# First FFN in 64-row tiles, groups of four chunk pairs, o copied by halves on ScalarE, and a new start, in a fused convolution and FFN

## The chip, the cores and the metric

One core of one Trainium2 chip. The time is device microseconds of the whole launch, the median of several runs. The profile comes from one such run; its span is about 1 to 2 us below the time of its run. PE is the tensor engine, DVE the vector engine, ACT the scalar engine, POOL the general one, SP the engine that issues many of the transfers. A ratio of two kernels is the mean time of one kernel's runs over that of the other's in the same rounds, so it is not quite the ratio of the medians quoted beside it.

## The reference

```python
# x: 8 x 4096 x 192, weight_gen: 8 x 4096 x 8 heads x 7 taps, w_in: 192 x 2048, w_out: 2048 x 192
w = softmax(weight_gen, axis=-1)
y[b, s, h, :] = sum_k w[b, s, h, k] * x_padded[b, s + k, h, :]     # causal, 24 channels a head
out = (relu(y @ w_in) ** 2) @ w_out                                # float32, 32768 tokens
```

## The kernel before

Tokens go in 64 blocks of 512. For a block: a band matrix per head is made on DVE (`st_band`), the convolution is a product of x with it on PE (`st_conv`, into a PSUM tile `yp`), ACT copies it to `y`. The first FFN has 2048 outputs in 16 chunks of 128, taken as 8 chunk pairs; each pair has a PSUM tile `h` of two banks, one for each half of the tokens. ACT makes the relu (`t`), DVE the square (`g`), and the second FFN adds `g` times `w_out` into a PSUM tile `o` of two banks, again one for each token half. There are three buffers for `h` and `yp` together and one for `o`; these fill the eight banks. The softmax runs in slices beside it, one batch ahead.

```python
    ps_h = ctx.enter_context(tc.tile_pool(name="ps_h", bufs=3, space=bass.MemoryType.PSUM))
    ps_o = ctx.enter_context(tc.tile_pool(name="ps_o", bufs=1, space=bass.MemoryType.PSUM))
    ...
    def st_mm1_lower(j, fps):            # rows 0 to 127 of w_in
        ...
                for half in range(2):
                    nc.tensor.matmul(
                        out=h[:, half, jj, :],
                        lhsT=w_a[:, fc * P : (fc + 1) * P],
                        rhs=y[:, half * TH : (half + 1) * TH], ...
    def st_mm1_upper(j, fps):            # rows 128 to 191, two row tiles at once
        ...
                for half, r0 in enumerate((0, LO)):
                    nc.tensor.matmul(
                        out=h_t[(j, fp)][:, half, jj, :],
                        lhsT=w_b[r0 : r0 + LO, fc * P : (fc + 1) * P],
                        rhs=y[r0 : r0 + LO, TB : TB + TH], ...
                        tile_position=(r0, 0),
    ...
    def st_o_evac(j):                    # one copy of all of o, on DVE
        o_sb = p_os.tile([P, 2, 2 * Dm], f32, name="o_sb")
        nc.vector.tensor_copy(out=o_sb, in_=o_t[j][:, :, 0 : 2 * Dm])
        nc.sync.dma_start(...)
    ...
    G0, G1, G2 = (0, 1, 2), (3, 4, 5), (6, 7)
    LATE = (5, 6, 7)
    # the loop over blocks, PE's part of it:
            st_mm1_lower(j, G0); st_mm1_upper(j, G0)
            if j: st_mm2(j - 1, LATE)
            ...
            st_mm1_lower(j, G1); st_mm1_upper(j, G1)
            st_mm2(j, (0, 1, 2))
            ...
            st_mm1_lower(j, G2)
            st_conv(j + 1); st_y_evac(j + 1)
            st_mm1_upper(j, G2)
            st_mm2(j, (3, 4))
```

The softmax here doesn't subtract the row's maximum and nothing guards it: scores larger than these inputs give would overflow.

## Time and profile before

| | before |
|---|---|
| time, median | 820.3 us |
| PE, DVE, ACT busy | 96%, 78%, 68% of the span |
| block period in the middle | 12.144 us |
| first FFN matmul starts | 24.25 us |
| 64 block periods / all the rest | 777 us / 43 us |

The block period is the distance between the first convolution matmuls of two blocks, from the matmuls' starts in the trace, between 120 and 780 us. PE's busy share alone would not tell a reader what can be gained; the starts of the matmuls do. The lines are in the prediction below.

### The profile page before, as it was taken

How to read it: one execution, taken by the hardware profiler on the slowest of the kernel's cores; microseconds unless marked ns; L12 is line 12 of the kernel's file. 1: busy time of each engine (PE TensorE's matmuls, PEld its weight loads, DVE VectorE, ACT ScalarE, POOL GpSimd, SP SyncE). 2: the span in 40 equal slices, each digit the busy share in tenths (PEclk: the TensorE clock that was granted, in tenths of full speed). 3: DMA queues.
4: the chain of work that ended last, by engine and by line, in shares of the span. 5: the costliest groups of instructions: out<-in, count | busy, mean ns of one | idle time of the engine just before them, and what ended most of it. 6: DMA issues, size and time to landing. Idle time of an engine off the chain costs nothing.

```text
span 819.6 us, 27464 instructions
## 1 busy us (share of the span) xinstructions
PE 783.1 (96%) x12288; PEld 662.1 (81%) x12288; DVE 642.0 (78%) x1194; ACT 557.1 (68%) x628; POOL 90.4 (11%) x126
## 2 busy tenths in 40 slices
PE   0499999999999999999999999999999999999997
PEld 0278888888888888888888888888888888888886
DVE  3498878878888878887788877887788887676674
ACT  1377677766777767777776767777677776676665
POOL 7650100010000000001000010001000000000000
PEclk9799999999999999999999999999999999999999
DMA  5844443345333353433533344233433334333111
GB/s 117 166 73 82 104 91 66 50 71 140 53 69 61 65 135 61 71 51 79 133 50 65 67 118 83 60 53 69 137 67 58 61 69 80 61 71 50 46 40 40
DMA packets 123799, 63.17 MB, mean 77 GB/s; under 512 B 87713, under 2 KB 121120, under 8 KB 122912
## 3 DMA queue, kind: packets, MB, share of 16 engines
q0 software_dynamic: 44480, 17.57, 19.6%
q1 hardware_dynamic: 79200, 43.84, 18.6%
q8 instruction: 96, 1.57, 0.8%
q14 instruction: 23, 0.19, 0.1%
HBM read 49.60 MB, written 29.36 MB: 96 GB/s over the span
## 4 chain that ended last, share of the span: by engine, by line
PE 94%; DVE 1%; DMA 1%; ACT 1%; POOL 0%; issue 0%; SPq 0%; ACTq 0%; DVEq 0%
PE o L322 43%; PE h L291 27%; PE h L304 16%; PE yp L266 7%; DMA wg<-in_weight_gen_dram 1%; ACT t L333 0%; DVE o_sb L343 0%; DVE bd L229 0%; ACT ex L142 0%; DVE g L339 0%; POOL v_small L163 0%; DVE ssum L150 0%; DVE rcp L155 0%; SPq L177 0%; ACTq L142 0%
## 5 line engine op out<-in xcount | busy, mean ns | idle before, releaser
L333 ACT ACTIVATE t<-h 128x1024 f16<-128x1024 f32 x512 | 490.0, 1026 | 128.7 <-PE h L304 128.7
L339 DVE TENSOR_TENSOR g<-t 128x1024 f16<-128x1024 f16 x512 | 353.9, 692 | 144.2 <-ACT t L333 139.3
L322 PE MATMUL o<-w_o,g 128*128 128x192 f16 x4096 | 371.5, 247 | 1.5 <-DVE o_sb L343 1.5
L322 PEld LDWEIGHTS <-g 128*128 128x128 f16 x4096 | 328.4, 98 | 42.0 <-issue 35.5
L291 PE MATMUL h<-y,w_a 128*128 128x256 f16 x2048 | 260.9, 274 | 9.6 <-ACT t L333 8.7
L291 PEld LDWEIGHTS <-w_a 128*128 128x128 f16 x2048 | 197.7, 98 | 34.1 <-issue 10.4
L229 DVE TENSOR_TENSOR bd<-wr,mask 128x832 f16<-128x832 f16 (+2 forms) x320 | 170.8, 583 | 10.6 <-POOL mask L94 8.4
L304 PE MATMUL h<-y,w_b 64*128 64x256 f16 x2048 | 146.4, 273 | 0.0
L279 ACT CAST y<-yp 128x768 f16<-128x768 f32 x64 | 51.1, 798 | 113.7 <-PE yp L266 113.7
L304 PEld LDWEIGHTS <-w_b 64*128 64x128 f16 x2048 | 84.7, 95 | 41.9 <-issue 27.6
L218 POOL DMA_DIRECT2D xt<-in_x_dram x56 | 48.4, 864 | 564.0 <-PE yp L266 518.2
L266 PE MATMUL yp<-bd,xt 128*32 128x104 f16 (+14 forms) x4096 | 65.9, 209 | 20.8 <-DVE bd L229 20.7
L266 PEld LDWEIGHTS <-xt 128*32 128x32 f16 (+3 forms) x4096 | 54.2, 91 | 34.7 <-issue 23.7
L343 DVE COPY o_sb<-o 128x768 f32<-128x768 f32 x64 | 60.8, 950 | 1.0 <-PE o L322 1.0
L150 DVE TENSOR_REDUCE ssum<-ex 128x64 f32<-128x448 f32 (+4 forms) x51 | 26.3, 515 | 13.4 <-ACT ex L142 13.3
L142 ACT ACTIVATE ex<-wg 128x448 f32<-128x448 f32 (+4 forms) x51 | 27.5, 540 | 13.1 <-DMA wg<-in_weight_gen_dram 13.1
L163 DVE TENSOR_TENSOR v_big<-ex,rcp 128x112 f16<-128x112 f32 (+3 forms) x188 | 32.7, 236 | 1.6
L155 DVE RECIPROCAL rcp<-ssum 128x64 f32<-128x64 f32 (+4 forms) x51 | 23.9, 469 | 1.8
L163 POOL TENSOR_TENSOR v_small<-ex,rcp 128x84 f16<-128x84 f32 (+1 forms) x28 | 13.8, 523 | 18.1 <-ACT t L333 14.1
L210 POOL DMA_DIRECT2D xt<-in_x_dram x8 | 4.6, 580 | 78.4 <-PE yp L266 67.7
L90 POOL TENSOR_SCALAR_AFFINE_SELECT mask<-mask 128x208 f16<-128x208 f16 (+2 forms) x6 | 6.9, 1146 | 0.4
L94 POOL TENSOR_SCALAR_AFFINE_SELECT mask<-mask 128x208 f16<-128x208 f16 (+2 forms) x6 | 6.6, 1093 | 0.4
(15 smaller groups left out, 16.2 us busy)
## 6 DMA issues: line engine op xcount, KB each, us to landing
out_dram<-o_sb SPq DMA_DIRECT2D x64, 384.0 KB, 2.8
xt<-in_x_dram POOLq DMA_DIRECT2D x56, 240.0 KB, 4.2
wg<-in_weight_gen_dram SPq DMA_DIRECT2D x6, 1064.0 KB, 7.1
wr<-vd SPq DMA_DIRECT2D x56, 80.0 KB, 3.0
vd<-v_big SPq DMA_DIRECT2D x7, 512.0 KB, 4.1
wg<-in_weight_gen_dram SPq DMA_DIRECT2D x4, 392.0 KB, 6.1
xt<-in_x_dram POOLq DMA_DIRECT2D x8, 192.0 KB, 3.7
wg<-in_weight_gen_dram SPq DMA_DIRECT2D x1, 896.0 KB, 5.9
```

The costliest lines, as they stand in the source:

```text
L142: nc.scalar.activation(out=self.ex[:, lo:hi].rearrange("p r g k e -> p (r g) k e"), in_=self.wg[:, lo:hi].rearrange("p r (g e) k -> p (r g ...
L163: eng.tensor_tensor(out=bass.AP(tensor=v.tensor, offset=v.offset + lo * H * SL + lo % SL * 2 + g * SL * 2, ap=[list(v.ap[0]), [H * SL + 2, ...
L218: eng.dma_start(out=dst, in_=rows(src, t0 + BASE, width))
L229: nc.vector.tensor_tensor(out=bd_t[j][:, H * lo : H * hi].rearrange("p (g m c) -> p g m c", g=HP, c=2 * SL), in0=wr_t[j][:, i].unsqueeze(2 ...
L266: nc.tensor.matmul(out=yp[p0 : p0 + m, ci, col : col + b - a], lhsT=x_t[j][:, i, 32 * q : 32 * q + m], rhs=bd[:, h // 2, h % 2, a - lo : b ...
L279: nc.scalar.copy(out=y, in_=yp_t[j].rearrange("p a c -> p (a c)")[:, 0 : TB + TH])
L291: nc.tensor.matmul(out=h[:, half, jj, :], lhsT=w_a[:, fc * P : (fc + 1) * P], rhs=y[:, half * TH : (half + 1) * TH], start=(jj == 0), stop ...
L304: nc.tensor.matmul(out=h_t[(j, fp)][:, half, jj, :], lhsT=w_b[r0 : r0 + LO, fc * P : (fc + 1) * P], rhs=y[r0 : r0 + LO, TB : TB + TH], sta ...
L322: nc.tensor.matmul(out=o[:, half, cc * Dm : (cc + 1) * Dm], lhsT=g_t[(j, fp)][:, half, jj, cc * P : (cc + 1) * P], rhs=w_o[:, fc, :], star ...
L333: nc.scalar.activation(out=t1, in_=h_t[(j, fp)], func=ActF.Relu)
L339: nc.vector.tensor_tensor(out=g, in0=t1, in1=t1, op=AluOp.mult)
L343: nc.vector.tensor_copy(out=o_sb, in_=o_t[j][:, :, 0 : 2 * Dm])
```

## The change

Its intent: every matmul of the first FFN in 64-row tiles, so that chunk pairs need no change of mode between two parts; groups of four pairs instead of three, three and two; the copy of `o` moved from busy DVE to ACT, by token halves, each as soon as its half is complete; and a start that loads weights sooner, splits the first softmax in three and runs 48 matmuls of zeros to bring PE's clock up.

```diff
-    p_t1 = ctx.enter_context(tc.tile_pool(name="p_t1", bufs=4))
-    p_g = ctx.enter_context(tc.tile_pool(name="p_g", bufs=6))
+    p_t1 = ctx.enter_context(tc.tile_pool(name="p_t1", bufs=6))
+    p_g = ctx.enter_context(tc.tile_pool(name="p_g", bufs=10))
...
+    def st_mm1(j, fp):
+        h = ps_h.tile([P, 2, 2, TH], f32, name="h", tag="h")
+        h_t[(j, fp)] = h
+        for jj in range(2):
+            fc = 2 * fp + jj
+            for k in range(NK):                          # NK = 3
+                for half, r0 in enumerate((0, RT)):      # RT = 64
+                    nc.tensor.matmul(
+                        out=h[:, half, jj, :],
+                        lhsT=w_i[r0 : r0 + RT, k, fc * P : (fc + 1) * P],
+                        rhs=y_t[j][r0 : r0 + RT, k, :],
+                        start=(jj == 0 and k == 0), stop=(k == NK - 1),
+                        tile_position=(r0, 0), ...
...
+    G0, G1 = (0, 1, 2, 3), (4, 5, 6, 7)
+        for i in range(48):                              # before the first block
+            nc.tensor.matmul(out=wp[:, 0:TB], lhsT=warm[:, 0:P], rhs=warm, ...)
...
+        for j in range(NBLK):
+            late = j in (0, 2)
+            ...            st_conv(j + 1); st_y_evac(j + 1)
+            for fp in G0:
+                st_mm1(j, fp); st_relu(j, fp); st_sq(j, fp)
+            if j:
+                for half in (0, 1):
+                    st_mm2(j - 1, G1, (half,))
+                    o_copy(j - 1, half, nc.scalar.copy)
+                o_store(j - 1, (0, 1), nc.sync)
+            ...            # bands of block j + 2, the softmax part
+            for fp in G1:
+                st_mm1(j, fp); st_relu(j, fp); st_sq(j, fp)
+            st_mm2(j, G0)
+            if late:
+                st_bands(j + 2, BANDS)
```

The convolution is laid out so that `y` has rows of 64 in each half, with 72 matmuls in place of 64. Cut: the loading of `w_in` into 64 rows and its copy to the other 64, one band mask for all tiles, the softmax in parts of 8, 8 and 16 rows.

More of the change, by code (lines that the diff above doesn't have):

```diff
@@ L49 @@
     TH = TB // 2
+    RT = 64
+    NK = D // RT
     NT = 5
@@ L55 @@
     bounds = [0, 104, 208, 304, 400, TB]
+    shifts = [lo - s for lo, s in zip(bounds, starts)]
     AluOp = mybir.AluOpType
@@ L73, with band_mask, copy_w_in @@
     ps_o = ctx.enter_context(tc.tile_pool(name="ps_o", bufs=1, space=bass.MemoryType.PSUM))
-    w_a = const.tile([P, Dff], f16, name="w_a")
-    w_b = const.tile([P, Dff], f16, name="w_b")
+    w_i = const.tile([P, NK, Dff], f16, name="w_i")
     w_o = const.tile([P, NF, Dm], f16, name="w_o")
-    mask = const.tile([P, TB, 2], f16, name="mask")
-    mask0 = const.tile([P, bounds[1], 2], f16, name="mask0")
-    R0 = 8
-    v_big = const.tile([P, R + 2 * (KK - 1), HP, SL, 2], f16, name="v_big")
-    v_small = [
-        const.tile([P, R0 + 2 * (KK - 1), HP, SL, 2], f16, name=f"v_small{i}") for i in range(2)
-    ]
-    def band_mask(t, shift):
-        n = t.shape[1]
-        nc.gpsimd.memset(t, 1.0)
-        nc.gpsimd.affine_select(
-            out=t, in_=t, pattern=[[1, n], [0, 2]], compare_op=AluOp.is_ge, fill=0.0,
-            base=shift, channel_multiplier=-1,
-        )
-        nc.gpsimd.affine_select(
-            out=t, in_=t, pattern=[[-1, n], [0, 2]], compare_op=AluOp.is_ge, fill=0.0,
-            base=KK - 1 - shift, channel_multiplier=1,
-        )
-    def load_w_in():
-        nc.gpsimd.dma_start(out=w_a, in_=moe_w_in[0:P, :])
-        for r0 in (0, LO):
-            nc.gpsimd.dma_start(out=w_b[r0 : r0 + LO, :], in_=moe_w_in[P:D, :])
+    mask = const.tile([P, P, 2], f16, name="mask")
+    FIRST = (8, 8, 16)
+    v_big = const.tile([P, R + 2 * HALO, HP, SL, 2], f16, name="v_big")
+    v_first = [
+        const.tile([P, r + 2 * HALO, HP, SL, 2], f16, name=f"v_first{i}")
+        for i, r in enumerate(FIRST)
+    ]
+    def band_mask():
+        nc.gpsimd.memset(mask, 1.0)
+        for sign, base in ((1, 0), (-1, KK - 1)):
+            nc.gpsimd.affine_select(
+                out=mask, in_=mask, pattern=[[sign, P], [0, 2]], compare_op=AluOp.is_ge,
+                fill=0.0, base=base, channel_multiplier=-sign,
+            )
+    WQ = 4
+    def load_w_in():
+        src = moe_w_in.rearrange("(k p) f -> p k f", p=RT)
+        for q in range(WQ):
+            c = slice(q * Dff // WQ, (q + 1) * Dff // WQ)
+            nc.gpsimd.dma_start(out=w_i[0:RT, :, c], in_=src[:, :, c])
+    def copy_w_in(q):
+        c = slice(q * Dff // WQ, (q + 1) * Dff // WQ)
+        nc.sync.dma_start(out=w_i[RT:P, :, c], in_=w_i[0:RT, :, c])
     def load_w_out():
@@ L186, in new_vd @@
         return vd_t[b]
-    x_t, wr_t, bd_t, yp_t, y_t, g_t, h_t, t1_t, o_t = ({} for _ in range(9))
+    x_t, wr_t, bd_t, yp_t, y_t, g_t, h_t, t1_t, o_t, o_sb_t = ({} for _ in range(10))
     def rows(ap2d, t0, width):
@@ L196, in rows, with block_load, x_load, wr_load @@
         )
-    def st_load(j):
-        b, t0 = j // NBB, (j % NBB) * TB
-        xt = p_x.tile([P, NT, D], f16, name="xt")
-        wr = p_wr.tile([P, NT, HP, SL * 2], f16, name="wr")
-        x_t[j], wr_t[j] = xt, wr
-        wr2 = wr.rearrange("p t g c -> p t (g c)")
-        vd = vd_t[b]
-        for dst, src, width, eng in (
-            (wr2, vd, H * SL, nc.sync),
-            (xt, x[b], D, nc.gpsimd),
-        ):
-            if t0 == 0:
-                eng.dma_start(out=dst[:, 0], in_=src[0:P, :])
-                first = rows(src, BASE + STEP, width)
-                first = bass.AP(
-                    tensor=first.tensor, offset=first.offset,
-                    ap=[first.ap[0], [STEP * width, NT - 1], first.ap[2]],
-                )
-                eng.dma_start(out=dst[:, 1:NT], in_=first)
-            else:
-                eng.dma_start(out=dst, in_=rows(src, t0 + BASE, width))
+    def block_load(j, dst, src, width, eng):
+        t0 = (j % NBB) * TB
+        if t0 == 0:
+            eng.dma_start(out=dst[:, 0], in_=src[0:P, :])
+            later = rows(src, BASE + STEP, width)
+            later = bass.AP(
+                tensor=later.tensor, offset=later.offset,
+                ap=[later.ap[0], [STEP * width, NT - 1], later.ap[2]],
+            )
+            eng.dma_start(out=dst[:, 1:NT], in_=later)
+        else:
+            eng.dma_start(out=dst, in_=rows(src, t0 + BASE, width))
+    def x_load(j):
+        x_t[j] = p_x.tile([P, NT, D], f16, name="xt")
+        block_load(j, x_t[j], x[j // NBB], D, nc.gpsimd)
+    def wr_load(j):
+        wr_t[j] = p_wr.tile([P, NT, HP, SL * 2], f16, name="wr")
+        block_load(
+            j, wr_t[j].rearrange("p t g c -> p t (g c)"), vd_t[j // NBB], H * SL, nc.sync
+        )
     def st_band(j, i):
@@ L224, in st_band @@
         n = hi - lo
-        m = mask[:, lo:hi]
-        if i == 0 and j % NBB == 0:
-            m = mask0
+        shift = 0 if i == 0 and j % NBB == 0 else shifts[i]
+        m = mask[:, shift : shift + n]
         shape = (P, HP, n // SL, 2 * SL)
@@ L242, in conv_pieces @@
     def conv_pieces():
-        for i in range(NT):
-            lo, hi = bounds[i], bounds[i + 1]
-            for later in (True, False):
-                for q in range(4):
-                    yield later, i, q, 32 * q, 0, lo, lo, hi
-                for half in (0, 1):
-                    a, b = max(lo, TH * half), min(hi, TH * (half + 1))
-                    if a < b:
-                        for q in (4, 5):
-                            yield later, i, q, 32 * (q - 4) + LO * half, 1, a - TH * half, a, b
+        pieces = []
+        for half in (0, 1):
+            a, b = TH * half, TH * (half + 1)
+            pieces.append([
+                (i, half, max(bounds[i], a), min(bounds[i + 1], b))
+                for i in range(NT) if bounds[i] < b and bounds[i + 1] > a
+            ])
+        for pair in zip(*pieces):
+            for later in (True, False):
+                for q in range(0, 2 * NK, 2):
+                    for i, half, a, b in pair:
+                        for qq in (q, q + 1):
+                            yield later, i, qq, half, a, b
     def st_conv_alloc(j):
-        yp_t[j] = ps_h.tile([P, 2, TB], f32, name="yp", tag="h")
+        yp_t[j] = ps_h.tile([P, 2 * TB], f32, name="yp", tag="h")
     def st_conv(j):
-        yp = yp_t[j]
-        for later, i, q, p0, ci, col, a, b in conv_pieces():
+        for later, i, q, half, a, b in conv_pieces():
             lo, hi = bounds[i], bounds[i + 1]
@@ L265, in st_conv @@
             bd = bd_t[j][:, H * lo : H * hi].rearrange("p (g c e) -> p g e c", g=HP, e=2)
+            p0 = RT * half + 32 * (q % 2)
+            col = TH * (q // 2) - TH * half
             nc.tensor.matmul(
-                out=yp[p0 : p0 + m, ci, col : col + b - a],
+                out=yp_t[j][p0 : p0 + m, col + a : col + b],
                 lhsT=x_t[j][:, i, 32 * q : 32 * q + m],
@@ L276, in st_y_evac, with st_mm2 @@
     def st_y_evac(j):
-        y = p_y.tile([P, TB + TH], f16, name="y")
+        y = p_y.tile([P, NK, TH], f16, name="y")
         y_t[j] = y
-        nc.scalar.copy(out=y, in_=yp_t[j].rearrange("p a c -> p (a c)")[:, 0 : TB + TH])
-    def st_mm1_lower(j, fps):
-        y = y_t[j]
-        for fp in fps:
-            h = ps_h.tile([P, 2, 2, TH], f32, name="h", tag="h")
-            h_t[(j, fp)] = h
-            for jj in range(2):
-                fc = 2 * fp + jj
-                for half in range(2):
+        nc.scalar.copy(
+            out=y, in_=yp_t[j][:, 0 : NK * TH].rearrange("p (k c) -> p k c", k=NK)
+        )
+    def st_mm1(j, fp):
[5 more added lines that the diff above has]
+                for half, r0 in enumerate((0, RT)):
                     nc.tensor.matmul(
                         out=h[:, half, jj, :],
-                        lhsT=w_a[:, fc * P : (fc + 1) * P],
-                        rhs=y[:, half * TH : (half + 1) * TH],
-                        start=(jj == 0), stop=False, skip_group_check=True,
-                    )
-    def st_mm1_upper(j, fps):
-        y = y_t[j]
-        for fp in fps:
-            for jj in range(2):
-                fc = 2 * fp + jj
-                for half, r0 in enumerate((0, LO)):
-                    nc.tensor.matmul(
-                        out=h_t[(j, fp)][:, half, jj, :],
-                        lhsT=w_b[r0 : r0 + LO, fc * P : (fc + 1) * P],
-                        rhs=y[r0 : r0 + LO, TB : TB + TH],
-                        start=False, stop=(jj == 1), skip_group_check=True,
+                        lhsT=w_i[r0 : r0 + RT, k, fc * P : (fc + 1) * P],
+                        rhs=y_t[j][r0 : r0 + RT, k, :],
+                        start=(jj == 0 and k == 0), stop=(k == NK - 1),
+                        skip_group_check=True,
                         tile_position=(r0, 0),
                     )
-    def st_mm2(j, fps):
+    def st_mm2(j, fps, halves=(0, 1)):
         if fps[0] == 0:
@@ L319, in st_mm2 @@
                 fc = 2 * fp + jj
-                for c in range(TB // P):
-                    half, cc = c // 2, c % 2
-                    nc.tensor.matmul(
-                        out=o[:, half, cc * Dm : (cc + 1) * Dm],
-                        lhsT=g_t[(j, fp)][:, half, jj, cc * P : (cc + 1) * P],
-                        rhs=w_o[:, fc, :],
-                        start=(fc == 0 and cc == 0), stop=(fc == NF - 1),
-                        skip_group_check=True,
-                    )
+                for half in halves:
+                    for cc in range(2):
+                        nc.tensor.matmul(
+                            out=o[:, half, cc * Dm : (cc + 1) * Dm],
+                            lhsT=g_t[(j, fp)][:, half, jj, cc * P : (cc + 1) * P],
+                            rhs=w_o[:, fc, :],
+                            start=(fc == 0 and cc == 0), stop=(fc == NF - 1),
+                            skip_group_check=True,
+                        )
     def st_relu(j, fp):
@@ L339, in st_sq @@
         nc.vector.tensor_tensor(out=g, in0=t1, in1=t1, op=AluOp.mult)
-    def st_o_evac(j):
-        o_sb = p_os.tile([P, 2, 2 * Dm], f32, name="o_sb")
-        nc.vector.tensor_copy(out=o_sb, in_=o_t[j][:, :, 0 : 2 * Dm])
-        nc.sync.dma_start(
-            out=out[j * TB : (j + 1) * TB, :].rearrange("(c p) d -> p c d", p=P),
-            in_=o_sb.rearrange("p a (b d) -> p (a b) d", b=2),
-        )
-    def softmax_whole(s, engines):
-        s.exp(0, s.rh)
-        s.recip(0, s.rh)
-        for n, lo in enumerate(range(0, s.rh, SL)):
-            s.scale(lo, min(lo + SL, s.rh), engines[n % len(engines)])
-        s.store(nc.sync)
@@ L358, with o_copy, o_store @@
-    G0, G1, G2 = (0, 1, 2), (3, 4, 5), (6, 7)
-    LATE = (5, 6, 7)
+    def o_copy(j, half, copy):
+        if half == 0:
+            o_sb_t[j] = p_os.tile([P, 2, 2 * Dm], f32, name="o_sb")
+        copy(out=o_sb_t[j][:, half], in_=o_t[j][:, half, 0 : 2 * Dm])
+    def o_store(j, halves, eng):
+        n = len(halves) * TH
+        t0 = j * TB + halves[0] * TH
+        eng.dma_start(
+            out=out[t0 : t0 + n, :].rearrange("(c p) d -> p c d", p=P),
+            in_=o_sb_t[j][:, halves[0] : halves[-1] + 1].rearrange(
+                "p a (b d) -> p (a b) d", b=2
+            ),
+        )
@@ L360, with st_bands @@
+    def st_bands(j, tiles):
+        if j < NBLK:
+            for i in tiles:
+                st_band(j, i)
+    G0, G1 = (0, 1, 2, 3), (4, 5, 6, 7)
     UNIT = 4
+    BANDS = (0, 2, 1, 3, 4)
     with nc.allow_low_precision("fp16 matmul pipeline"), tc.manual_schedule():
         vd0 = new_vd(0)
-        parts = [Softmax(0, P * R0 * i, R0, v_small[i % 2], vd0) for i in range(S // (P * R0))]
-        parts[0].load(nc.sync)
-        nc.vector.memset(v_small[0], 0.0)
-        band_mask(mask0, 0)
@@ L369 @@
-        softmax_whole(parts[0], (nc.vector, nc.gpsimd))
-        st_load(0)
-        load_w_in()
-        for i in range(1, NT):
-            band_mask(mask[:, bounds[i] : bounds[i + 1]], bounds[i] - starts[i])
-        parts[1].load(nc.sync)
-        st_load(1)
-        nc.vector.memset(v_small[1], 0.0)
-        for i in range(NT):
-            st_band(0, i)
+        parts = [
+            Softmax(0, P * sum(FIRST[:i]), r, v_first[i], vd0) for i, r in enumerate(FIRST)
+        ]
+        warm = const.tile([P, TB], f16, name="warm")
@@ new lines @@
+        nc.vector.memset(warm, 0.0)
+        for i in (0, 1):
+            parts[i].load(nc.sync)
+            nc.vector.memset(v_first[i], 0.0)
+        wp = ps_h.tile([P, 2 * TB], f32, name="wp", tag="h")
+        for i in range(48):
+            nc.tensor.matmul(
+                out=wp[:, 0:TB], lhsT=warm[:, 0:P], rhs=warm, start=True, stop=True
+            )
+        x_load(0)
+        load_w_in()
+        band_mask()
+        for i in (0, 1):
+            s = parts[i]
+            s.exp(0, s.rh)
+            s.recip(0, s.rh)
+            s.scale(0, s.rh, nc.vector)
+            s.store(nc.sync)
+            if i == 0:
+                wr_load(0)
+                wr_load(1)
+                copy_w_in(0)
+                copy_w_in(1)
@@ L379 @@
+        copy_w_in(2)
+        copy_w_in(3)
+        parts[2].load(nc.sync)
+        x_load(1)
+        load_w_out()
+        st_bands(0, BANDS)
         st_conv_alloc(0)
@@ L381 @@
         st_y_evac(0)
-        load_w_out()
-        band_mask(mask[:, 0 : bounds[1]], -starts[0])
-        softmax_whole(parts[1], (nc.gpsimd,))
-        for s in parts[2:]:
-            s.load(nc.sync)
-        st_load(2)
-        nc.vector.memset(v_big, 0.0)
-        nxt, done = None, 0
-        if B > 1:
-            nxt = Softmax(1, 0, R, v_big, new_vd(1))
-            nxt.load(nc.sync)
-        for j in range(NBLK):
-            b, jb = j // NBB, j % NBB
-            more = j + 1 < NBLK
-            if j < 2:
-                softmax_whole(parts[2 + j], (nc.gpsimd,))
-            if nxt and jb == 5:
-                nxt.store(nc.sync)
-                nxt, done = None, 0
-                if b + 2 < B:
-                    nxt = Softmax(b + 2, 0, R, v_big, new_vd(b + 2))
-                    nxt.load(nc.sync)
-            lo = hi = 0
-            if nxt and jb != 5:
-                left = (4 - jb) % NBB + 1
-                lo = done
-                hi = done = min(lo + -(-(nxt.rh - lo) // (UNIT * left)) * UNIT, nxt.rh)
+        nc.gpsimd.memset(v_first[2], 0.0)
@@ new lines, with spread @@
+        nc.gpsimd.memset(v_big, 0.0)
+        x_load(2)
+        wr_load(2)
+        plan = {}
+        def spread(b, rh, blocks):
+            lo = 0
+            for n, j in enumerate(blocks):
+                left = len(blocks) - n
+                hi = min(lo + -(-(rh - lo) // (UNIT * left)) * UNIT, rh)
+                if lo < hi:
+                    plan[j] = (b, lo, hi)
+                lo = hi
+        spread(0, parts[2].rh, (0, 1))
+        for b in range(1, B):
+            first = NBB * (b - 1)
+            spread(b, R + HALO, range(first + (2 if b == 1 else -2), first + 5))
@@ L410 @@
+        rows_of = {0: parts[2]}
+        for j in range(NBLK):
+            nb, lo, hi = plan.get(j, (None, 0, 0))
+            after = plan.get(j + 1)
+            if after and after[1] == 0:
+                s = Softmax(after[0], 0, R, v_big, new_vd(after[0]))
+                s.load(nc.sync)
+                rows_of[after[0]] = s
             if j + 3 < NBLK:
-                st_load(j + 3)
-            st_mm1_lower(j, G0)
-            st_mm1_upper(j, G0)
+                x_load(j + 3)
+            late = j in (0, 2)
@@ L415 @@
             if j:
-                st_mm2(j - 1, LATE)
-            for fp in G0:
-                st_relu(j, fp)
-            if lo < hi:
-                nxt.exp(lo, hi)
-            if more:
-                for i in (0, 1, 2):
-                    st_band(j + 1, i)
-            st_sq(j, 0)
-            st_sq(j, 1)
-            if j:
-                st_o_evac(j - 1)
-            st_sq(j, 2)
-            if more:
-                for i in (3, 4):
-                    st_band(j + 1, i)
-            st_mm1_lower(j, G1)
@@ L434 @@
-            st_mm1_upper(j, G1)
-            st_mm2(j, (0, 1, 2))
-            for fp in G1:
+                if j + 1 < NBLK:
+                    st_conv_alloc(j + 1)
+                    st_conv(j + 1)
+                    st_y_evac(j + 1)
+                if not late:
+                    st_bands(j + 2, BANDS[0:3])
+            else:
+                st_bands(1, BANDS[0:3])
+            for fp in G0:
+                st_mm1(j, fp)
                 st_relu(j, fp)
                 st_sq(j, fp)
-            if lo < hi:
-                nxt.recip(lo, hi)
-                nxt.scale(lo, hi, nc.vector)
@@ L443 @@
-            if more:
-                st_conv_alloc(j + 1)
-            st_mm1_lower(j, G2)
-            if more:
-                st_conv(j + 1)
-                st_y_evac(j + 1)
-            st_mm1_upper(j, G2)
-            st_mm2(j, (3, 4))
-            for fp in G2:
+            if j:
+                for half in (0, 1):
+                    st_mm2(j - 1, G1, (half,))
+                    o_copy(j - 1, half, nc.scalar.copy)
+                o_store(j - 1, (0, 1), nc.sync)
+            elif NBLK > 1:
+                st_bands(1, BANDS[3:5])
+                st_conv_alloc(1)
+                st_conv(1)
+                st_y_evac(1)
@@ L452 @@
+            if not late:
+                st_bands(j + 2, BANDS[3:5])
+            if hi:
+                s = rows_of[nb]
+                s.exp(lo, hi)
+                s.recip(lo, hi)
+                s.scale(lo, hi, nc.vector)
+                if hi == s.rh:
+                    s.store(nc.sync)
+            for fp in G1:
+                st_mm1(j, fp)
                 st_relu(j, fp)
                 st_sq(j, fp)
-        st_mm2(NBLK - 1, LATE)
-        st_o_evac(NBLK - 1)
+            st_mm2(j, G0)
@@ L459 @@
+            if late:
+                st_bands(j + 2, BANDS)
+            if j + 3 < NBLK:
+                wr_load(j + 3)
+        st_mm2(NBLK - 1, G1, (0,))
+        o_copy(NBLK - 1, 0, nc.scalar.copy)
+        st_mm2(NBLK - 1, G1, (1,))
+        o_store(NBLK - 1, (0,), nc.sync)
+        o_copy(NBLK - 1, 1, nc.vector.tensor_copy)
+        o_store(NBLK - 1, (1,), nc.scalar)
 _INS = ['x', 'weight_gen', 'moe_w_in', 'moe_w_out']
```

## The prediction

> **What bounds the kernel now.** I read the page's busy table first, then the costliest groups, then the order of time of one block in the middle, then the first 45 us. Busy table and groups (busy us, mean ns; idle us before, releaser):
>
> ```profile
> PE 783.1 (96%) x12288; PEld 662.1 (81%) x12288; DVE 642.0 (78%) x1194; ACT 557.1 (68%) x628; POOL 90.4 (11%) x126
> ...
> L322 PE MATMUL o<-w_o,g 128*128 128x192 f16 x4096 | 371.5, 247 | 1.5 <-DVE o_sb L343 1.5
> L291 PE MATMUL h<-y,w_a 128*128 128x256 f16 x2048 | 260.9, 274 | 9.6 <-ACT t L333 8.7
> L304 PE MATMUL h<-y,w_b 64*128 64x256 f16 x2048 | 146.4, 273 | 0.0
> ```
>
> PE hardly ever waits: 1.5 us before second-FFN matmuls, 9.6 before first-FFN ones, 8.7 of that a single wait. So the steady part is set by how fast matmuls start. The mean of 247 to 274 ns is latency, not rate; the rate is in the order of time (start us, length us, what), one block of PE alone:
>
> ```profile
> 400.91 1.53 PE L291 MATMUL h<-y,w_a 128*128 128x256 f16 x12
> 402.36 0.83 PE L304 MATMUL h<-y,w_b 64*128 64x256 f16 x12
> 403.13 2.15 PE L322 MATMUL o<-w_o,g 128*128 128x192 f16 x24
> 405.12 1.47 PE L291 MATMUL h<-y,w_a 128*128 128x256 f16 x12
> 406.52 0.83 PE L304 MATMUL h<-y,w_b 64*128 64x256 f16 x12
> 407.28 2.15 PE L322 MATMUL o<-w_o,g 128*128 128x192 f16 x24
> 409.27 1.04 PE L291 MATMUL h<-y,w_a 128*128 128x256 f16 x8
> 410.24 1.00 PE L266 MATMUL yp<-bd,xt 128*32 128x104 f16 x64
> 411.17 0.61 PE L304 MATMUL h<-y,w_b 64*128 64x256 f16 x8
> 411.71 1.50 PE L322 MATMUL o<-w_o,g 128*128 128x192 f16 x16
> ```
>
> From the single starts in the trace, between 66 and 800 us: inside a run a 256-column matmul starts every 109.2 ns, a pair of 64-row ones (two 4 ns apart) also every 109, a 192-column one every 82.5. Where the array's partition changes, more passes: full rows to 64 rows 204 ns (95 too many, and the next pair is 12 late), 64 rows to full 201 against 105 (96, and 11 more on the next), full to the convolution's column tiles 202 (93), these to 64 rows 144 where the last stage needs 48 (96, and 12). A block has seven such changes: two each in its first two groups and three around the convolution. That is 2 x (107 + 107) + 93 + 108 + 107 = 0.74 us. Check: 48 x 0.109 + 64 x 0.0825 + convolution 0.84 + 0.74 = 12.1 us; blocks do repeat every 12.14 us. So 64 blocks are 777 us, and about 42 us of the 819.6 are start and end. The start:
>
> ```profile
> 16.82 0.53 PE L266 MATMUL yp<-bd,xt 128*32 128x104 f16 x12 [16.82 <-DVE bd L229]
> ...
> 24.25 2.72 PE L291 MATMUL h<-y,w_a 128*128 128x256 f16 x12 [0.89 <-ACT y L279]
> ...
> 35.06 0.93 ACT L142 ACTIVATE ex<-wg 128x784 f32<-128x784 f32 x1 [10.03 <-DMA wg<-in_weight_gen_dram]
> 35.90 2.83 ACT L333 ACTIVATE t<-h 128x1024 f16<-128x1024 f32 x3
> ...
> 36.96 2.84 PE L291 MATMUL h<-y,w_a 128*128 128x256 f16 x12 [8.68 <-ACT t L333]
> ```
>
> First FFN matmul at 24.25. Then ACT, in order, holds the first relu behind an exp whose weights come late: PE loses 8.7 us. Both early runs of 12 take 2.7 to 2.8 us where 1.3 would do, so the clock was half: 1.3 + 0.7 + 1.4 + 0.7 us and a little, 4.4 in all.
>
> **What the Trainium skill says.** "TensorEngine Tiling (Array Packing)", Key Properties: changing the tiling mode, not merely the tile, drains the TensorE. It gives no figure; this trace agrees and shows 93 to 109 ns per change. The same page, Gotcha 1: different row tiles must write different PSUM banks; before and after both give each token half its own bank. "TensorE: Matmul & The Clock Gate", Back-to-back issue gap: N / 2.4 + 2.5 ns once warm, that is 109.2 and 82.5 for 256 and 192 columns; the trace has exactly these, with every weight load hidden. The same page, Part 1: the array starts at half clock and about 3.4 us of activity release it; the doubled durations above agree.
>
> **The change part by part.**
>
> *First FFN.* 192 rows were 128 + 64; they become 3 x 64. Per block 32 full matmuls and 32 in 16 pairs become 96 in 48 pairs. 48 x 109 = 5.24 us, the same as before: the tiling itself saves nothing. Second FFN: 64 x 82.5, unchanged.
>
> *Changes of mode.* A block is now convolution, 48 tiled, 32 full, 48 tiled, 32 full. Five changes: 109 + 107 + 107 + 107 + 93 = 0.52 us. Saved: 0.21 us a block.
>
> *Convolution.* 64 matmuls become 72, in 18 stages of four column tiles. A stage of 104 columns passed in 46 ns before; now six stages each of 104, 104, 112 wide: 6 x (46 + 46 + 49) = 0.845 us. Before: 0.84. Nothing.
>
> Sum: 5.24 + 5.28 + 0.85 + 0.52 = **11.89 us a block**, if ACT and DVE keep up. I lay that out from the block's first convolution matmul. y copy (0.80) 1.07 to 1.87. First h from 0.96, one per 0.655. A relu starts 0.31 after its last matmul's start, lasts 1.03, follows the next by 0.915: 1.83, 2.75, 3.66, 4.58. There are three h buffers: the fourth h needs the first relu done and 0.05 more; by my sums it is ready 0.03 us in time. Tight, but no wait. The two o copies (384 columns each, about 0.46 by the slope from 0.80 at 768 to 1.03 at 1024) fit at 5.5 and 6.6. exp: 0.63 for 8 rows. Second group's first relu could start at 7.31, and after an 8-row exp at 7.47: PE waits about 0.13. With 18 such blocks and the larger exps of blocks 2 to 4: 4 us in all. DVE loses the o copy (0.95) and has 5.5 + 2.65 + 2.0 = 10.2 us of work in 11.9; its results are there over 3 us ahead. So 64 x 11.9 = 762 us, and 4 of waits.
>
> *Start.* POOL no longer scales and masks ahead of the w_in loads, so those go out near 2 to 4 us instead of 10. The first part's scaling is wholly on DVE: 8 calls of about 0.3 us instead of 4. First store near 9.3 (8.3 before), wr loads from 11, landing in 3 to 4 us because w_in is out of the way (5.7 before); five bands, convolution and y copy as before: first FFN matmul at about **18.6** (24.25). The 48 warm-up matmuls (512 columns, 216 ns warm, 427 cold, estimates from the formula above) end near 14, so the array is warm and nothing is delayed. The 8.7 us wait goes: the last softmax part is first needed in block 0's second half.
>
> *New waits in the start.* In block 0 the second convolution waits for two bands that stand on DVE behind four squares, and the third for all bands of block 2, behind exp, 3 us of scaling and four squares: block 0 takes about 16.4, 4.5 too long. Block 2 has its bands last again, behind 16 rows (4 us of DVE): PE idles 4.3 us. I allow 1 us for a clock that falls in such a gap.
>
> *End.* The last o is copied and stored by halves: about 4.0 us after the last matmul instead of 4.6. Against 64 full blocks the last one lacks a convolution (-1.0) and 32 matmuls follow (+2.75).
>
> Sum: 18.6 + 762 + 4.5 + 4.3 + 4 + 1.75 + 4.0 + 1 = 800 us span; the measured times are 1 us above the span before: 801. I round to 800, as block periods came out at 11.89.
>
> **Rivals.**
>
> (a) *ACT takes PE's place.* ACT gains o copies: 8 x 0.915 + 0.8 + 0.92 + 0.5 = 9.6 of 11.9, so not by its sum. For it: only three h buffers with runs of four, margin 0.03. If each run loses 0.15, 128 x 0.15 = 19 us: 819, the same as before. Against: in the present block the same three buffers cost one 0.056 us wait.
>
> (b) *The changes of mode are no drain but weight loads that can't be hidden, or tiles of 64 rows lose their 109 ns in a long run.* Then the first FFN grows: at 115 a pair, 48 x 6 ns x 64 = 18 us. Against: runs of six pairs hold 109 to the end.
>
> (c) *The start gains less.* If wr loads land behind w_in and its copies, first FFN matmul at 22 and clock cold in block 0: 806.
>
> (d) *Start without my new waits*, bands hidden: 792.
>
> **Range and chances.** Period uncertain by 0.05 us (3 us), waits by 4, start by 5: 800, **792 to 809**. The 2% line is 804.2; 4 us below it against a spread of some 6 to 7: faster 0.72, same 0.27, slower 0.01.
>
> **What would show it.** Block period 11.9 in the middle (11.7 or 12.1 refutes my count of five changes); 109 ns in tiled runs; about 95 + 12 ns at five places a block; waits of PE for t under 5 us in all after 100 us; first FFN matmul at 18.6; gaps of some 3 us for bands before the convolutions of blocks 1, 2 and 4; full clock from 10 us on. Wrong if PE waits for ACT in every run of four, or the convolution of 72 costs over 0.95.

## The result, and the profile after

The changed kernel takes **865.5 us** (863.7 to 866.5, four runs) against 820.3 (four runs): ratio 1.0546, 95% interval 1.0522 to 1.0569. It is 5.5% slower; 2.5% faster was predicted.

| | before | after |
|---|---|---|
| time | 820.3 | 865.5 |
| block period | 12.144 | 12.823 (median; mean 12.855) |
| 64 periods (mean) / the rest | 777 / 43 | 823 / 43 |
| first FFN matmul | 24.25 | 22.74 |
| PE, DVE, ACT busy | 96, 78, 68% | 92, 69, 70% |

So the start is no faster as a whole and the loss lies in the middle, in each block. The busy table, the chain that ended last and the costliest groups of the page, after:

```profile
PE 789.4 (92%) x14896; PEld 682.2 (79%) x14896; DVE 592.2 (69%) x1159; ACT 604.4 (70%) x753; POOL 69.4 (8%) x86
...
PE 62%; issue 16%; ACT 16%; DVE 3%; DMA 2%; ACTq 0%; SPq 0%; DVEq 0%
...
L334 ACT ACTIVATE t<-h 128x1024 f16<-128x1024 f32 x512 | 483.0, 1029 | 10.0 <-PE h L304 9.5
...
L323 PE MATMUL o<-w_o,g 128*128 128x192 f16 x4096 | 370.3, 246 | 53.8 <-ACT o_sb L345 53.8
L304 PE MATMUL h<-y,w_i 64*128 64x256 f16 x6144 | 364.6, 271 | 1.4 <-ACT y L293 0.9
```

ACT is busier by 47 us (604 against 557), DVE is less busy by 50, and PE is busy for the same time: 789 us against 783, of which 12 are the warm-up. What is new is one entry, 53.8 us of PE idle before second-FFN matmuls (1.5 before), ended by ACT's copy of `o`. The first FFN, which holds all the 64-row tiles, waits 1.4 us in all. ACT's share of the chain went from 1% to 16%, of which the page puts 12% down to the relus and 3% to the copies: the copy of half 0 stands on ACT behind the group's fourth relu. The same in the order of time, one block of PE and the copies (start us, length us, what; in brackets idle before and what ended it):

```profile
409.40 1.50 PE L323 MATMUL o<-w_o,g 128*128 128x192 f16 x16
...
411.18 0.51 ACT L345 COPY o_sb<-o 128x384 f32<-128x384 f32 x1
...
411.74 1.48 PE L323 MATMUL o<-w_o,g 128*128 128x192 f16 x16 [0.84 <-ACT o_sb L345]
...
413.16 2.79 PE L304 MATMUL h<-y,w_i 64*128 64x256 f16 x48
413.26 0.48 ACT L345 COPY o_sb<-o 128x384 f32<-128x384 f32 x1 [1.57 <-PE o L323]
...
415.88 2.81 PE L323 MATMUL o<-w_o,g 128*128 128x192 f16 x32
```

The 16 matmuls of half 0 start from 409.40 on. Sixteen more of half 1 should follow at 410.73; they start at 411.74, just as the copy of half 0 is done (411.69). They write the other bank of `o` and don't need that copy. The distance from the last start of half 0 to the first of half 1 is 1.09 us where within a run it is 0.082. The 0.84 in brackets is less than the 1.01 us lost because matmul ends are modelled: the loss is read from starts, 411.74 - 410.73 = 1.01. The trace has 64 such gaps, one for each block, and they add up to 64 us. The listing of the compiled program has the wait, at the first matmul of half 1 and nowhere else in the run of 32:

```
5088 L323 Matmult o<-w_o,g 128x192
5090 L323 Matmult o<-w_o,g 128x192 [waits Activation_49]
5092 L323 Matmult o<-w_o,g 128x192
```

The program makes its own waits from the accesses to tiles: the copy reads the tile `o`, the next matmul writes the tile `o`, and the two were put in order though their banks differ. The start:

```profile
9.11 0.33 SPq L187 DMA_DIRECT2D vd<-v_first  x1
...
13.88 0.33 SPq L211 DMA_DIRECT2D wr<-vd  x1
...
19.13 0.27 PE L280 MATMUL yp<-bd,xt 128*32 128x104 f16 x2 [5.84 <-DVE bd L239]
...
22.74 5.63 PE L304 MATMUL h<-y,w_i 64*128 64x256 f16 x48 [0.89 <-ACT y L293]
```

The first softmax store goes out at 9.11 but what reads it only at 13.88: it took 4.8 us to land. (Before: 8.27 and 10.00.) The warm-up ended at 13.3 us, PE stood idle for 5.8 us, and the trace's clock record falls to half at 18.0: the first 48 first-FFN matmuls take 5.6 us where later ones take 2.8.

### The profile page after: what moved, and what is told of

The parts are those of the page before. It is cut to its first block, busy times and chain, and to the rows that moved or that the text cites. A ratio compares the mean times of both kernels' runs of the same rounds, so it can differ in the third digit from the quotient of the medians.

```text
span 862.0 us, 32753 instructions
## 1 busy us (share of the span) xinstructions
PE 789.4 (92%) x14896; PEld 682.2 (79%) x14896; DVE 592.2 (69%) x1159; ACT 604.4 (70%) x753; POOL 69.4 (8%) x86
## 3 DMA queue, kind: packets, MB, share of 16 engines
q0 software_dynamic: 45008, 17.31, 18.6%
## 4 chain that ended last, share of the span: by engine, by line
PE 62%; issue 16%; ACT 16%; DVE 3%; DMA 2%; ACTq 0%; SPq 0%; DVEq 0%
PE o L323 31%; PE h L304 26%; ACT t L334 12%; PE yp L280 6%; ACT o_sb L345 3%; DVE bd L239 1%; DMA wr<-vd 1%; DVE g L340 1%; DMA vd<-v_first 1%; ACT ex L152 0%; DVE ssum L160 0%; DVE v_first L173 0%; DVE rcp L165 0%; DMA wg<-in_weight_gen_dram 0%; DVE v_big L173 0%
## 5 line engine op out<-in xcount | busy, mean ns | idle before, releaser
L334 ACT ACTIVATE t<-h 128x1024 f16<-128x1024 f32 x512 | 483.0, 1029 | 10.0 <-PE h L304 9.5
L340 DVE TENSOR_TENSOR g<-t 128x1024 f16<-128x1024 f16 x512 | 346.2, 690 | 190.4 <-ACT t L334 190.1
L323 PE MATMUL o<-w_o,g 128*128 128x192 f16 x4096 | 370.3, 246 | 53.8 <-ACT o_sb L345 53.8
L304 PE MATMUL h<-y,w_i 64*128 64x256 f16 x6144 | 364.6, 271 | 1.4 <-ACT y L293 0.9
L304 PEld LDWEIGHTS <-w_i 64*128 64x128 f16 x6144 | 292.9, 95 | 53.2 <-issue 11.5
L345 ACT COPY o_sb<-o 128x384 f32<-128x384 f32 x127 | 62.8, 494 | 101.0 <-PE o L323 101.0
L160 DVE TENSOR_REDUCE ssum<-ex 128x64 f32<-128x448 f32 (+6 forms) x49 | 25.9, 530 | 57.7 <-ACT ex L152 57.7
L152 ACT ACTIVATE ex<-wg 128x448 f32<-128x448 f32 (+6 forms) x49 | 26.4, 539 | 2.6 <-DMA wg<-in_weight_gen_dram 2.6
L165 DVE RECIPROCAL rcp<-ssum 128x64 f32<-128x64 f32 (+6 forms) x49 | 23.3, 476 | 1.7
L380 PE MATMUL wp<-warm 128*128 128x512 f16 x48 | 12.0, 417 | 1.3 <-DVE warm L373 1.3
L173 DVE TENSOR_TENSOR v_first<-ex,rcp 128x112 f16<-128x112 f32 (+2 forms) x32 | 6.3, 269 | 0.2
```

The source lines that it names most:

```text
L152: nc.scalar.activation(out=self.ex[:, lo:hi].rearrange("p r g k e -> p (r g) k e"), in_=self.wg[:, lo:hi].rearrange("p r (g e) k -> p (r g ...
L160: nc.vector.tensor_reduce(out=ssum.rearrange("p r g e -> p (r g) e"), in_=self.ex[:, lo:hi].rearrange("p r g k e -> p (r g) e k"), axis=Ax ...
L173: eng.tensor_tensor(out=bass.AP(tensor=v.tensor, offset=v.offset + lo * H * SL + lo % SL * 2 + g * SL * 2, ap=[list(v.ap[0]), [H * SL + 2, ...
L304: nc.tensor.matmul(out=h[:, half, jj, :], lhsT=w_i[r0 : r0 + RT, k, fc * P : (fc + 1) * P], rhs=y_t[j][r0 : r0 + RT, k, :], start=(jj == 0 ...
L323: nc.tensor.matmul(out=o[:, half, cc * Dm : (cc + 1) * Dm], lhsT=g_t[(j, fp)][:, half, jj, cc * P : (cc + 1) * P], rhs=w_o[:, fc, :], star ...
L334: nc.scalar.activation(out=t1, in_=h_t[(j, fp)], func=ActF.Relu)
```

## The experiments

**The theory:** the whole loss is the wait of half 1's first matmul for ACT's copy of half 0, and everything else about as predicted. **Rivals:** ACT, which is busy 47 us longer than before (604 against 557), bounds the block by its load; or 64-row tiles or the changes of mode cost more than counted. Nine kernels ran; all give correct results.

### Two o tiles

```diff
-            o_t[j] = ps_o.tile([P, 2, TB], f32, name="o")
+            o_t[j] = [ps_o.tile([P, TB], f32, name=f"o{i}") for i in range(2)]
...
-                            out=o[:, half, cc * Dm : (cc + 1) * Dm],
+                            out=o[half][:, cc * Dm : (cc + 1) * Dm],
-        copy(out=o_sb_t[j][:, half], in_=o_t[j][:, half, 0 : 2 * Dm])
+        copy(out=o_sb_t[j][:, half], in_=o_t[j][half][:, 0 : 2 * Dm])
```

> The changed kernel, with the PSUM tile o of two banks made into two tiles of one bank; every instruction and its order stay. Theory: the loss is one wait a block, the first second-FFN matmul of token half 1 waiting for ACT's copy of half 0 (1.01 us between two starts instead of 0.08, 63 times). Then the block period falls from 12.82 to about 11.8 and the time from 865.5 to about 800. Rival, ACT's added copies bound the block themselves: ACT's work is the same here, so the time stays at about 860. Rival, 64-row tiles or more mode changes cost it: also about 860.

Measured: **801.2 us**, 0.9749 of before (0.9734 to 0.9763). Same instructions, same order, same engines; the listing shows no wait on ACT there. The period is 11.817 (median; mean 11.844), 1.006 less; 64 x 1.006 = 64.4 us, and the times differ by 64.4. The costliest groups and the order of time of this run:

```profile
L323 PE MATMUL o<-w_o,g 128*128 128x192 f16 x4096 | 360.1, 246 | 0.0
```

```profile
406.40 2.81 PE L323 MATMUL o<-w_o,g 128*128 128x192 f16 x32
...
408.18 0.51 ACT L345 COPY o_sb<-o 128x384 f32<-128x384 f32 x1
...
409.15 2.90 PE L304 MATMUL h<-y,w_i 64*128 64x256 f16 x48
409.25 0.48 ACT L345 COPY o_sb<-o 128x384 f32<-128x384 f32 x1 [0.56 <-PE o L323]
```

The 32 matmuls now go as one run, the first copy lies beside it. ACT is busy as before the edit (604.7 against 604.4 us), so its load was not the bound. Both rivals fall.

### Copies after both halves

```diff
                 for half in (0, 1):
                     st_mm2(j - 1, G1, (half,))
+                for half in (0, 1):
                     o_copy(j - 1, half, nc.scalar.copy)
```

> The changed kernel, one o tile as it is, but both copies of o issued after the matmuls of both halves. Theory (the wait is made by a copy between the two halves): it is gone here too; ACT gets to the second group's relus later, so a wait of about 0.1 to 0.5 us for an h buffer may come in its place in blocks with an exp: 800 to 812. Rival, ACT is too busy: about 860.

Measured: 817.0 us, 0.9936 of before (0.9919 to 0.9952). The wait between the halves is gone (starts within runs of the second FFN are at most 94 ns apart, but for one wait of 0.7 us in the tail after the loop, which this edit left), which agrees with the theory. But 817 is above the 812 expected. Each wait that came in its place is as large as expected: 0.16 to 0.48 us in the 42 blocks with an exp between 100 and 780 us, none in the others. They add up to 14 us there; it is the sum that I had mis-sized. Where it went, from the order of time:

```profile
406.84 0.86 ACT L345 COPY o_sb<-o 128x384 f32<-128x384 f32 x2 [0.94 <-PE o L323]
407.58 0.63 ACT L152 ACTIVATE ex<-wg 128x448 f32<-128x448 f32 x1
408.10 3.77 ACT L334 ACTIVATE t<-h 128x1024 f16<-128x1024 f32 x4
...
409.18 0.83 PE L304 MATMUL h<-y,w_i 64*128 64x256 f16 x12 [0.31 <-ACT t L334]
```

Two copies and an exp now stand together ahead of the relus; the fourth chunk pair of the group needs the buffer of the first and finds its relu too late. The mean period is 12.076 here, 0.23 above that with two tiles: 15 us of the 15.8. So copying early was a sound idea; it needed two tiles.

### The same wait, longer

```diff
-                    o_copy(j - 1, half, nc.scalar.copy)
+                    o_copy(j - 1, half, nc.vector.tensor_copy)
```

> The changed kernel with its one o tile, but the two copies of o put on DVE instead of ACT. A dose of the same wait: on DVE the first copy stands behind the fourth square of the group, which ends at 412.04 us in the block traced, and takes about 0.56; so the second half's matmuls start at about 412.65 instead of 411.74, against 410.72 without a wait. Theory: the wait grows from 1.01 to about 1.9 us, the period from 12.82 to about 13.7, the time from 865 to about 922. Rival, ACT's load is what costs: ACT is lighter here by about 1 us a block, so the time falls towards 800.

Measured: 914.6 us, 1.1142 of before (1.1112 to 1.1172). One block of this run:

```profile
429.58 1.50 PE L323 MATMUL o<-w_o,g 128*128 128x192 f16 x16
...
432.13 0.55 DVE L345 COPY o_sb<-o 128x384 f32<-128x384 f32 x1
432.74 1.48 PE L323 MATMUL o<-w_o,g 128*128 128x192 f16 x16 [1.67 <-DVE o_sb L345]
```

The gap between the halves is 1.92 us instead of 1.09 and the period 13.643 instead of 12.823: 0.82 each. ACT is lighter here and the time 49 us longer. The time follows the wait, not the load of ACT. (922 was expected; the copy started a little sooner behind its square than I had added up.)

### The tiles alone

The kernel before, with the first FFN and the layout of the convolution of the changed one, all else as it was (groups of three, three and two, one copy of `o` on DVE, the old start).

```diff
-            st_mm1_lower(j, G0)
-            st_mm1_upper(j, G0)
+            for fp in G0:
+                st_mm1(j, fp)
...                                  # likewise G1
-            st_mm1_lower(j, G2)
             if more:
                 st_conv(j + 1)
                 st_y_evac(j + 1)
-            st_mm1_upper(j, G2)
+            for fp in G2:
+                st_mm1(j, fp)
```

> The kernel before with only the first FFN in 64-row tiles (and the convolution laid out for them); groups of three, three and two, o copy on DVE, start as before. My count of mode changes gives seven a block as before and 48 pairs at 109 ns, so a period of 12.1 to 12.2 and 818 to 826 us. If the tiles by themselves save time: about 805. If they cost it (over 109 ns a pair in longer runs): 835 or more.

Measured: 813.9 us, 0.9904 of before (0.9889 to 0.9919); period 12.030. That is less than the 818 to 826 expected. So the tiles, with the layout of the convolution that they bring, don't cost; they gain 0.114 us a block, which I had put at nothing. From the starts: the convolution's matmuls span 0.730 us instead of 0.794 (0.064), and the first FFN's wait for an `h` buffer, 0.05 us a block before, is gone. The pairs still start every 109 ns and there are still seven changes of mode a block.

### The start

Four kernels on top of the two `o` tiles (801.2 us, 0.9749).

```diff
-        for i in range(48):          # no warm-up: the loop and its tile are taken out
+        for i in range(75):          # or a longer one
```

> The changed kernel with two o tiles (801.2) without the 48 warm-up matmuls. Theory: they end at 13.3 us, PE is then idle to 19.1, the clock falls at 18.3 and the first FFN runs at half speed all the same; so they are worth nothing: within 1.5 us of 801. Rival: they pay: 804 or more.

Measured: 802.4 us, 0.9763 (0.9743 to 0.9782).

> The same with 75 warm-up matmuls instead of 48, so that they end near 19 us, when the first convolution can start. Theory: the clock stays full and block 0's first 48 first-FFN matmuls take 2.8 us instead of 5.6: 796 to 798.5. Rival: the gaps in block 0 let the clock fall anyway, or the warm-up now delays the convolution: 800 to 803.

Measured: 800.9 us, 0.9738 (0.9713 to 0.9764). The three intervals overlap: in the means no worth of the warm-up can be seen, whether it is absent, ends too early, or lasts to the convolution (19.9 us). With 75 the clock of the profiled run (801.96 us) held to 23.1 us and fell then, within block 0. But the six runs with 75 spread from 797.5 to 802.9 us, and in order of time their granted clocks are 1.0, 0.995, 0.994 and three times 0.991: two runs, at 797.5 and 798.0, are as fast as expected, and they are those with the highest clock. So the warm-up may pay 4 to 5 us in runs in which the clock holds; no profile shows one of them, and this is not shown.

```diff
-        x_load(1)
-        load_w_out()
+        nc.gpsimd.memset(v_first[2], 0.0)
+        nc.gpsimd.memset(v_big, 0.0)
         st_bands(0, BANDS)
+        held = const.tile([P, 2], f16, name="held")
+        nc.gpsimd.tensor_copy(out=held, in_=bd_t[0][:, 0:2])   # POOL waits for the first band
+        x_load(1)
+        load_w_out()
...                                  # the two memsets leave their place after st_y_evac(0)
```

> The same with 48 warm-up matmuls, but the loads of w_o and of block 1's x held back until block 0's first band is made. Theory: the first store of the softmax landed 4.8 us after its issue (1.4 in the kernel before) because w_in, x and w_o packets fill the DMA engines; with two of the three gone the wr loads are issued near 12 instead of 13.9 us and the first FFN matmul starts near 20 instead of 22.9: 798 to 800. Rival, w_in alone fills them: no gain, 801.

Measured: **797.5 us**, 0.9707 (0.9689 to 0.9726). The gain is there but not by the step I had named: the wr loads are issued at 13.39 instead of 13.88, so the store still takes over 4 us with these two loads out of the way; that the packets of `w_in` alone do this, as the rival says, was not tested. What shortened is the next hop: the first convolution matmul starts at 15.67, 2.3 us after that issue, where it started 5.3 us after it (13.88 to 19.13) in the changed kernel. Block 0's first 48 matmuls of the first FFN, and the convolution of block 2:

```profile
19.88 5.27 PE L304 MATMUL h<-y,w_i 64*128 64x256 f16 x48 [0.89 <-ACT y L293]
...
36.21 1.10 PE L280 MATMUL yp<-bd,xt 128*32 128x104 f16 x26 [0.62 <-DVE bd L239]
```

> Both: loads held back and 64 warm-up matmuls (ending near 16.7 us). If the two gains add: 793 to 796. If one makes the other useless: 797 to 800.

Measured: 797.0 us, 0.9703 (0.9682 to 0.9725): in the mean the warm-up adds nothing here either. The profiled run:

```profile
19.61 2.80 PE L304 MATMUL h<-y,w_i 64*128 64x256 f16 x48 [0.92 <-ACT y L293]
...
35.93 0.22 PE L280 MATMUL yp<-bd,xt 128*32 128x104 f16 x2 [1.44 <-DVE bd L239]
```

The longer warm-up put off the first convolution (17.75 us against 15.67) but not the first FFN. In this run block 0's first FFN did go at full clock, 2.80 us for 48 matmuls instead of 5.27, yet the convolution of block 2 starts at 35.93 instead of 36.21 us: the 2.5 us that PE gained came to 0.3. In both, that convolution waits for its bands on DVE (0.6 and 1.4 us idle before it). So in this pair of profiles PE's clock does not set the end of block 0; the bands do. It is one pair, and the profiled run (798.96 us) is one of the two slow ones of five: the others took 795.3, 795.5 and 797.0, with clocks of 0.998, 0.995 and 0.995 against 0.994 and 0.991. In it the clock fell again at 37.2 us, and block 2's first 48 matmuls took 3.83 us where they took 2.79 with the loads held back alone.

### A version that beats both

In blocks 0 and 2 the bands for two blocks ahead stood last on DVE, behind the softmax part and four squares.

```diff
+            if late:                         # now ahead of the softmax part
+                st_bands(j + 2, BANDS)
             if hi:
                 s = rows_of[nb]
...
-            if late:                         # at the end of the block
-                st_bands(j + 2, BANDS)
```

> The best so far (two o tiles, loads held back, 797.5) with the bands that blocks 0 and 2 make last put ahead of the softmax part of the same block. Theory: convolution 4 no longer waits (2.9 and 3.3 us lost in blocks 2 and 3) and convolution 2 waits less (about 1): 790 to 793. Rival: the squares that now come later are missed by the second FFN and the gain is given back: 796 to 798.

Measured: **790.4 us**, 0.9622 of before (0.9599 to 0.9645): the fastest, 3.8% below the kernel before. The convolution of block 4 starts at 60.72 instead of 64.29 us and that of block 5 at 72.85 instead of 79.31. The start of block 4 with the loads held back alone, and here:

```profile
64.29 0.22 PE L280 MATMUL yp<-bd,xt 128*32 128x104 f16 x2 [2.23 <-DVE bd L239]
...
66.85 4.00 PE L304 MATMUL h<-y,w_i 64*128 64x256 f16 x48
```

```profile
60.72 0.94 PE L280 MATMUL yp<-bd,xt 128*32 128x104 f16 x72
61.59 2.79 PE L304 MATMUL h<-y,w_i 64*128 64x256 f16 x48
```

PE's wait for bands over the whole run fell to 3.8 us, from 8.7 with the loads held back (11.7 with two tiles alone). Part of the gain goes with the clock: in the first run it was half from 65.9 to 69.4 us, after that wait; here it is full from 31.1 us on.

## Why the prediction was wrong

**The step that failed** is in the layout of a block, where it says "The two o copies (384 columns each, about 0.46 by the slope from 0.80 at 768 to 1.03 at 1024) fit at 5.5 and 6.6." Their lengths (0.48 to 0.51) and places were about right. I asked whether ACT has time for the copies and not who waits for them: I let half 1's matmuls run on while half 0 is copied, and in this program they wait. That is worth 1.006 us a block, 64 us in all. Rival (a) had named ACT, and a loss of 0.15 us per run of four from late `h` buffers; after has 0.3 us of such waits by the profile's count, and some 3 us by the starts (18 blocks of 0.09 and four early ones of 0.2 to 0.5). So none of my rivals was this one. The prediction's last line names "PE waits for ACT in every run of four" as a sign of being wrong: PE did wait for ACT, but once a block and for a copy. It was to be seen beforehand: the listing of the compiled program, which needs no run, shows the wait.

**The rest, step by step**, with the wait removed (two tiles, 801.2 against 800 predicted):

- Changes of mode, 0.74 us before and 0.52 after, saving 0.21: right. Each of the five changes, of four kinds, costs what was read off before: second FFN to tiles 178 ns between starts instead of 82.5, and the second pair 11 late; tiles to second FFN 202 and 93; second FFN to convolution 176; convolution to tiles 144. Tiles alone, with seven, 12.030; tiles in groups of four, with five, 11.817: the difference is 0.213. These two kernels differ in more than that, but the starts give the same for the two changes fewer: 108 + 107 ns.
- First FFN "5.24 us, the same as before": right, pairs keep 109 ns in runs of 24. (The section that the prediction quotes, Back-to-back issue gap, calls its formula the gap of an isolated matmul and says that a stream with weight loads departs from it. Here every matmul has its weight load, and the starts keep to the formula.)
- Convolution, "Nothing": 0.064 us a block was gained. That alone brings the sum of 11.89 to 11.82, as measured; the old wait for `h`, 0.05 us a block, was not in that sum.
- Waits of ACT, "4 us in all": by the starts 2.9 us. The 18 blocks foreseen wait 0.09 us each instead of 0.13, and blocks 2 to 5, with the larger exps, 0.2 to 0.5.
- Start, "about 18.6": 22.7 to 22.9. The store landed late, which was my rival (c), and the clock was low in block 0, where I had counted on full clock from 10 us on. What that cost stays open (see The start).
- New waits in the start: right in kind (gaps before the convolutions of blocks 1, 2 and 4). Block 0, put at 16.4 us, took 16.4 (22.93 to 39.29). Against 11.82 us, the stretches from convolution 3 to 4 and from 4 to 5 last 14.70 and 15.16 us, 6.2 too long, where I had 4.3 and 1 for a falling clock; the clock did fall there, and block 4's first 48 matmuls took 4.26 us instead of 2.79.
- The start's misses and the shorter period cancel, so 801 next to 800 is partly luck.

What stays open: what the warm-up is worth when the clock holds (the fastest runs with 75 and with 64 matmuls are 5.5 and 3.7 us below the slowest of the same kernel, and none of them was profiled), and in a start that PE bounds; and which of the two loads held back, `w_o` or `x`, let the wr loads land some 3 us sooner (no run took them apart).

## What to carry to other kernels

When a change puts a reader between two writers of one on-chip tile, look in the compiled program for the wait that this makes, even if they use different banks; give parts that are meant to overlap their own tiles. An engine with time to spare can still hold up another: ask of each moved instruction who waits for it, not only whether it fits. And where a block is paced by one engine's data, a faster other engine can gain little: in the pair of profiles above, block 0 waits for bands on DVE, and of 2.5 us that PE gained 0.3 were left.

## What the Trainium skill lacked or had wrong

- "TensorEngine Tiling (Array Packing)", Key Properties, says that a change of the tiling mode drains the engine, with no figure. Here 93 to 97 ns go per change, and up to 12 more on the next start; two changes fewer a block gave 0.213 us.
- "PSUM — Partial Sum Buffer", Summary: rules for kernel authors, advises to read a bank other than the one being written. That alone did not let copy and matmul overlap: with two banks in one tile the matmul waited 1.01 us for the copy, with two tiles not at all. No page that I read warns of it.
- No page that I read says what a warm-up of PE is worth inside a kernel whose first block waits for another engine. Here one that lasted to the first convolution gave 800.9 us against 802.4 without any, which is within the noise, with single runs from 797.5 to 802.9.
